# Weights in parts through one queue, cast, turned and multiplied on chip before the gate, in the start of a recurrent attention and maxout kernel

## The chip, the cores and the metric

One core of a Trainium2 chip (trn2). The metric is the device time of one execution in microseconds (us); fast executions of one kernel lie within about 1.5% of each other (159.77 to 161.48 in seven of the kernel before, 155.39 to 156.37 in four of the changed one). Profiles show one execution; their *span* runs from the first to the last instruction and is about 1.7 us shorter than the time. Some executions fall in a slow state, and one of the kernel before took 200.93 us. Medians are over all executions of a run; ratios and verdicts use its fast ones only.

## The reference, cut to what matters

```python
# RWKV-6 like recurrence; B, H, S, D = 4, 8, 768, 48
for t in range(S):
    cur = einsum('bhd,bhe->bhde', u * k[t], v[t])
    y[t] = einsum('bhd,bhde->bhe', r[t], state + cur)
    state = w[t][..., None] * state + einsum('bhd,bhe->bhde', k[t], v[t])
x = y as (3072 tokens, 384)
out = maximum(x @ w1, x @ w2) @ w_out      # w1, w2: 384 x 1024; w_out: 1024 x 384
```

The kernel uses max(a, b) = b + relu(a - b): with wd = w1 - w2 and wc = w2 @ w_out, out = relu(x @ wd) @ w_out + x @ wc. So before the first *gate product* (x @ wd) all of wd must exist, and before the first output all of wc.

## The kernel before

The work is cut into 12 units (3 chunks of 256 positions x 4 batches). A schedule by hand, one long string of steps such as `cs.1` (step cs of unit 1), gives the order; each engine takes its own steps in this order. I count units from zero only inside step names; in prose unit `.0` is the first.

| steps | engine | what |
|---|---|---|
| w k r v, u | transfer queue | loads of a unit (384 KB each), and u to all partitions |
| lw, lp, cs, m, z, AO, AE, iA | ScalarE, GpSimd, TensorE, VectorE | log of the decay, pair sums, prefix sums, exponentials |
| rp, kp, tr, ev | VectorE, TensorE | decayed r and k, turned on TensorE, copied out |
| rk, rku, dg, vd, yb | GpSimd, VectorE, TensorE | the diagonal term r*u*k times v |
| kv, Sa, Tf, S1, sc, M, yi, ya, xT | all | state, scores, masks, output y, copied as bf16 |
| g, r, oc, oa, ob, os | TensorE, ScalarE | gate products, relu, two output products, copies |
| row, WL, Wt, dec, S0 | queue, ScalarE, GpSimd | decay of the state to the next chunk |

The parts that change:

```python
def w1(n):  nc.sync.dma_start(out=w1f, in_=rows(moe_w1))          # f32, plain queue
def w2(n):  nc.gpsimd.dma_start(out=w2_sb, in_=rows(moe_w2))      # cast to bf16 in transfer
def wo(n):  nc.gpsimd.dma_start(out=wo_sb, in_=rows(moe_w_out))   # cast to bf16 in transfer
def wd(ko): nc.vector.tensor_sub(wd_sb[:, ko, :], w1f[:, ko, :], w2_sb[:, ko, :])
def wt(ko): nc.sync.dma_start_transpose(out=w2T_sb[:, ko], in_=w2_sb[:, ko, :])
def wcm(ko): ... 8 matmuls of w2T_sb and wo_sb                    # 3 x 8 = 24 in all
def wce(ko): nc.vector.tensor_copy(wc_sb[:, ko, :], WC[ko])
def lp(n):  nc.gpsimd.tensor_add(t, lw[:, :, 0, :], lw[:, :, 1, :])
def ya(n):
    inter(n, 0)                      # term of the old state
    for i in range(2): ...           # masked scores times v
```

Of the kernel before, what the change touches and what calls it, by code (L numbers as in the profile page):

```python
# [553 lines left out]
```

## Time and profile before

| | |
|---|---|
| time, median of the first three runs | 161.64 us (160.17 to 200.93) |
| span of the profiled run | 158.9 us |
| first gate product starts | 28.47 us |
| TensorE busy before it / from it to the last copy | 8.82 of 28.47 / 126.39 of 126.96 us |
| from the last copy to the end | 3.47 us |

To be read as: a start of 28.5 us in which TensorE mostly waits, then a stretch in which it does nothing but work. The prediction shows the lines.

### The profile page before, as it was taken

How to read it: one execution, taken by the hardware profiler on the slowest of the kernel's cores; microseconds unless marked ns; L12 is line 12 of the kernel's file. 1: busy time of each engine (PE TensorE's matmuls, PEld its weight loads, DVE VectorE, ACT ScalarE, POOL GpSimd, SP SyncE). 2: the span in 40 equal slices, each digit the busy share in tenths (PEclk: the TensorE clock that was granted, in tenths of full speed). 3: DMA queues.
4: the chain of work that ended last, by engine and by line, in shares of the span. 5: the costliest groups of instructions: out<-in, count | busy, mean ns of one | idle time of the engine just before them, and what ended most of it. 6: DMA issues, size and time to landing. Idle time of an engine off the chain costs nothing.

```text
span 158.9 us, 6567 instructions
## 1 busy us (share of the span) xinstructions
PE 135.2 (85%) x2920; PEld 90.1 (57%) x2920; DVE 100.4 (63%) x168; ACT 96.9 (61%) x165; POOL 94.7 (60%) x91
## 2 busy tenths in 40 slices
PE   0402860899999999999899999999999999999991
PEld 0102440565676676766666767667667576586760
DVE  6345579848847859669377596693966956844000
ACT  3242322662397687857858679778587785774641
POOL 8556554808499299952976919958589395330000
PEclk9999999999999999999999999999999999999999
DMA  5999999999999950239496962999229520010402
GB/s 133 248 190 369 366 214 247 178 288 254 268 269 262 247 161 6 106 52 324 132 277 171 283 170 86 220 283 280 89 76 262 167 101 6 15 38 4 151 4 99
...
## 3 DMA queue, kind: packets, MB, share of 16 engines
...
## 4 chain that ended last, share of the span: by engine, by line
PE 82%; DMA 6%; DVE 4%; SPq 2%; POOL 2%; issue 2%; ACT 0%; ACTq 0%; DVEq 0%
PE go L474 22%; PE go L498 20%; PE go L493 9%; PE ex L239 6%; DMA lv<-in_v_dram 6%; PE sc L395 6%; PE y L457 4%; PE sc L327 4%; PE y L436 3%; PE go L219 3%; PE y L349 3%; DVE wd_sb L207 3%; PE y L418 2%; SPq L181 1%; DVE M L400 1%
## 5 line engine op out<-in xcount | busy, mean ns | idle before, releaser
L400 DVE TENSOR_TENSOR M<-sc,mask 128x512 bf16<-128x512 f32 x48 | 30.9, 686 | 17.8 <-PE sc L395 17.8
L474 PE MATMUL go<-xT,wd_sb 128*128 128x256 bf16 x288 | 37.6, 282 | 4.8 <-DVE wd_sb L207 4.3
L482 ACT ACTIVATE gT<-go 128x512 bf16<-128x512 f32 x48 | 27.9, 595 | 16.6 <-PE go L474 15.7
L474 PEld LDWEIGHTS <-wd_sb 128*128 128x128 bf16 x288 | 28.0, 100 | 13.3 <-DVE wd_sb L207 4.6
L498 PE MATMUL go<-wo_sb,gT 128*128 128x384 bf16 x192 | 35.5, 326 | 0.0
L299 POOL TENSOR_TENSOR rku<-lr,lk 128x768 f32<-128x768 f32 x12 | 21.8, 1813 | 8.6 <-DMA lr<-in_r_dram 8.6
L498 PEld LDWEIGHTS <-gT 128*128 128x128 bf16 x192 | 18.6, 98 | 12.3
L315 POOL TENSOR_TENSOR vd<-lv,dg 128x768 bf16<-128x768 f32 x12 | 17.7, 1476 | 12.0 <-DVE dg L310 11.8
L304 POOL TENSOR_TENSOR rku<-rku,u_b 128x768 f32<-128x768 f32 x12 | 21.8, 1813 | 2.6 <-DMA u_b<-in_u_dram 1.8
L239 PE MATMUL ex<-lp,triS 128*128 128x384 f32 x24 | 12.4, 603 | 7.0 <-POOL lp L235 7.0
L235 POOL TENSOR_TENSOR lp<-lw 128x384 f32<-128x384 f32 x12 | 12.0, 999 | 9.2 <-ACT lw L230 9.2
L265 ACT ACTIVATE ex<-mz 128x768 f32<-128x768 f32 x12 | 9.8, 814 | 10.5 <-DVE rn L269 10.5
L493 PE MATMUL go<-wc_sb,xT 128*128 128x384 bf16 x72 | 15.8, 329 | 0.0
L503 ACT COPY osb<-go 128x384 f32<-128x384 f32 x24 | 11.4, 476 | 7.1 <-PE go L498 7.1
L334 DVE COPY T<-sc 128x1024 bf16<-128x1024 bf16 x12 | 8.3, 689 | 11.7 <-PE sc L327 11.6
L230 ACT ACTIVATE lw<-lw 128x768 f32<-128x768 f32 x12 | 10.1, 838 | 8.8 <-DMA lw<-in_w_dram 8.8
L465 ACT CAST xT<-y 128x768 bf16<-128x768 f32 x12 | 12.2, 1020 | 4.5 <-PE y L457 4.5
L294 POOL CAST vn<-lv 128x768 bf16<-128x768 f32 x12 | 10.8, 905 | 3.8 <-DMA lv<-in_v_dram 3.8
L334 ACT COPY T<-sc 128x1024 bf16<-128x1024 bf16 x12 | 12.1, 1012 | 1.0 <-PE sc L327 0.3
L310 DVE TENSOR_REDUCE dg<-rku 128x16 f32<-128x768 f32 x12 | 11.4, 946 | 1.3 <-POOL rku L304 1.3
L269 DVE TENSOR_TENSOR rn<-lr,ex 128x768 bf16<-128x768 f32 x12 | 11.3, 945 | 1.1 <-ACT ex L261 1.1
L395 PE MATMUL sc<-T 48*64 48x128 bf16 x384 | 10.8, 229 | 1.1 <-DVE M L400 1.1
...
## 6 DMA issues: line engine op xcount, KB each, us to landing
...
```

Source lines behind the costliest of these rows:

```text
L239: nc.tensor.matmul(EX[:, 0, 0:HD], triS, U[n]["lp"].rearrange("p h d -> p (h d)"))
L299: nc.gpsimd.tensor_mul(t, U[n]["r"], U[n]["k"])
L304: nc.gpsimd.tensor_mul(t, t, u_b.rearrange("p (h d) -> p h d", h=H).unsqueeze(1).to_broadcast([P, 2, H, D]))
L315: nc.gpsimd.tensor_mul(t.rearrange("p i h d -> p h i d"), U[n]["v"], U[n]["dg"].to_broadcast([P, H, 2, D]))
L334: copy(t.rearrange("d j i p q -> d (j i p q)"), U[n]["tr"][b].rearrange("d j i p q -> d (j i p q)"))
L395: nc.tensor.matmul(sc[e][q, p, :], t[d, 1, i, p, :], t[d, 0, :, p, :])
L400: nc.vector.tensor_mul(U[n]["M", i][:, e], U[n]["sc", i][e], mask[:, i].rearrange("s i q -> s (i q)").unsqueeze(1).to_broadcast([P, NP, P]))
L465: nc.scalar.copy(t.rearrange("c b k (q i) -> c (b k) i q", i=2), U[n]["y"][:, :, 0:HD].rearrange("c b (k i q) -> c b k i q", k=KO, i=2))
L474: nc.tensor.matmul(g[:, f, :], wd_sb[:, ko, fo * P:(fo + 1) * P], U[n]["xT"][:, :, ko, :], start=(f == 0 and ko == 0), stop=(f == 1 and ko ...
L482: nc.scalar.activation(U[n]["gT"][:, 2 * j:2 * j + 2].rearrange("p f j t -> p (f j t)"), U[n]["g", j].rearrange("p f j t -> p (f j t)"), A ...
L493: nc.tensor.matmul(t, U[n]["xT"][:, b, ko, :], wc_sb[:, ko, :], start=(ko == 0), stop=False)
L498: nc.tensor.matmul(U[n]["o", b], U[n]["gT"][:, fo, b, :], wo_sb[:, fo, :], start=False, stop=(fo == FO - 1))
```

## The change

The intent is to shorten the start: load the weights as f32 parts through one queue in the order of need, cast them on chip, turn w2 on TensorE while it would wait, and make the wc products before the first gate product. Its core (cut; the whole order string is rewoven too, for all 12 units):

```diff
+    def wa(ko): nc.sync.dma_start(out=w1f[:, ko], in_=moe_w1[ko * P:(ko + 1) * P, :])
+    def wl(ko): nc.sync.dma_start(out=w2f[:, ko], in_=moe_w2[ko * P:(ko + 1) * P, :])
+    def wq(ko): nc.scalar.copy(w2_sb[:, ko, :], w2f[:, ko, :])
+    def wf(h):  nc.sync.dma_start(out=half(wof, h), in_=half(rows(moe_w_out), h))
+    def wh(h):  nc.gpsimd.tensor_copy(half(wo_sb, h), half(wof, h))
-    def wt(ko): nc.sync.dma_start_transpose(...)
+    def wtm(ko): 8 x nc.tensor.transpose(t[:, fo, :], w2_sb[:, ko, fo * P:(fo + 1) * P], ident)
+    def wte(ko): nc.scalar.copy(w2T_sb[:, ko] ..., WT[ko] ...)
     def wce(ko):
-        nc.vector.tensor_copy(wc_sb[:, ko, :], WC[ko])
+        nc.scalar.copy(wc_sb[:, ko, :], WC[ko])
     def lp(n):
+        eng = nc.vector if n in (0, 1) else nc.gpsimd
     def ya(n):
-        inter(n, 0)
         for i in range(2):
+            if i == 1: inter(n, 0)
-    for t in S_f + S_0: nc.vector.memset(t, 0.0)   # first chunk copies its state instead
 ... (order of the start, before)
-... ya.0 xT.0 w1 wd.1 wd.2 k.1 ... wt.0 lw.2 lp.2 wd.0 rp.1 iA.1 g0.0 ... wcm.0 wce.0 ... wcm.2 wce.2
+... ya.0 xT.0 r.1 rp.1 iA.1 wcm.2 wce.2 wa.2 wd.2 wcm.1 wce.1 row.1 k.1 ... tr.1 ... w.2 lw.2 lp.2 wcm.0 wce.0 g0.0
```

A routine `warm` (matmuls of zeros) is defined and not called.

More of the change, by code (lines that the diff above doesn't have):

```diff
@@ L17 @@
 ORDER = """
-w.0 k.0 r.0 u v.0 w.1 lw.0 w2 lp.0 cs.0 m.0 z.0 AO.0 AE.0 rp.0 row.0 iA.0 rk.0 rku.0 dg.0 vb.0
-vd.0 lw.1 lp.1 kp.0 kv.0 Sa.0 S1.0 Tf.0 tr.0 ev1.0 ev0.0 cs.1 m.1 z.1 AO.1 AE.1 yb.0 yi.0 sc0.0
-M0a.0 M0b.0 sc1.0 M1a.0 M1b.0 ya.0 xT.0 w1 wd.1 wd.2 k.1 r.1 v.1 w.2 wo rk.1 rku.1 vb.1 wt.0
-lw.2 lp.2 wd.0 rp.1 iA.1 g0.0 r0.0 dg.1 vd.1 g1.0 r1.0 g2.0 r2.0 kp.1 tr.1 ev1.1 ev0.1 kv.1 Sa.1
-Tf.1 S1.1 cs.2 m.2 g3.0 r3.0 yb.1 yi.1 sc1.1 M1a.1 M1b.1 z.2 AO.2 AE.2 wcm.0 wce.0 sc0.1 M0a.1
-M0b.1 wt.1 wcm.1 wce.1 wt.2 wcm.2 wce.2 k.2 r.2 v.2 w.3 rk.2 rku.2 vb.2 rp.2 iA.2 dg.2 vd.2 lw.3
@@ L24 @@
-lp.3 ya.1 xT.1 oc0.0 oa0.0 ob0.0 os0.0 oc1.0 oa1.0 ob1.0 os1.0 kp.2 tr.2 ev0.2 ev1.2 kv.2 Sa.2
-Tf.2 S1.2 g0.1 r0.1 g1.1 r1.1 k.3 r.3 v.3 rk.3 rku.3 w.4 vb.3 k.4 r.4 v.4 w.5 lw.4 lp.4 yb.2
-yi.2 sc1.2 M1a.2 M1b.2 cs.3 g2.1 g3.1 r2.1 r3.1 row.1 m.3 z.3 AO.3 AE.3 sc0.2 M0a.2 M0b.2 vb.4
-rp.3 iA.3 oc0.1 oa0.1 ob0.1 os0.1 WL.0 Wt.0 dec.0 S0.0 ya.2 xT.2 oc1.1 oa1.1 ob1.1 os1.1 dg.3
-vd.3 rk.4 rku.4 out1.0 kp.3 tr.3 ev1.3 ev0.3 kv.3 Sa.3 S1.3 Tf.3 g0.2 r0.2 g1.2 r1.2 yb.3 yi.3
-sc1.3 M1a.3 M1b.3 k.5 r.5 v.5 w.6 vb.5 cs.4 lw.5 lp.5 g2.2 r2.2 g3.2 r3.2 out0.0 row.2 m.4 z.4
@@ L30 @@
-AO.4 AE.4 WL.1 Wt.1 dec.1 S0.1 sc0.3 M0a.3 M0b.3 lw.6 lp.6 rp.4 iA.4 out1.1 oc0.2 oa0.2 ob0.2
-os0.2 oc1.2 oa1.2 out0.2 row.3 ya.3 xT.3 ob1.2 os1.2 dg.4 vd.4 rk.5 rku.5 kp.4 tr.4 ev0.4 ev1.4
-kv.4 Sa.4 S1.4 Tf.4 g0.3 r0.3 g1.3 r1.3 out0.1 yb.4 yi.4 sc1.4 M1a.4 M1b.4 cs.5 g2.3 r2.3 g3.3
-r3.3 m.5 z.5 AO.5 AE.5 sc0.4 M0a.4 M0b.4 rp.5 iA.5 oc0.3 oa0.3 ob0.3 os0.3 dg.5 vd.5 ya.4 xT.4
-row.4 WL.4 Wt.4 dec.4 WL.2 Wt.2 dec.2 S0.2 oc1.3 oa1.3 ob1.3 os1.3 kp.5 tr.5 ev0.5 kv.5 ev1.5
-Sa.5 S1.5 Tf.5 g0.4 r0.4 g1.4 r1.4 yb.5 yi.5 sc1.5 M1a.5 M1b.5 S0.4 cs.6 m.6 g2.4 r2.4 g3.4 r3.4
@@ L36 @@
-z.6 AO.6 AE.6 sc0.5 M0a.5 M0b.5 k.6 r.6 v.6 vb.6 w.7 rk.6 rku.6 lw.7 lp.7 rp.6 iA.6 out1.3 oc0.4
-oa0.4 ob0.4 os0.4 dg.6 vd.6 ya.5 xT.5 oc1.4 oa1.4 ob1.4 os1.4 kp.6 tr.6 ev0.6 ev1.6 kv.6 Sa.6
-S1.6 Tf.6 g0.5 r0.5 g1.5 r1.5 yb.6 yi.6 sc1.6 M1a.6 M1b.6 row.5 cs.7 m.7 g2.5 r2.5 g3.5 r3.5
-out1.2 z.7 AO.7 AE.7 sc0.6 M0a.6 M0b.6 k.7 r.7 v.7 w.8 vb.7 rk.7 rku.7 lw.8 lp.8 rp.7 iA.7 dg.7
-vd.7 oc0.5 oa0.5 ob0.5 os0.5 WL.3 Wt.3 dec.3 S0.3 ya.6 xT.6 out0.3 oc1.5 oa1.5 ob1.5 os1.5 kp.7
-tr.7 ev0.7 ev1.7 kv.7 Sa.7 S1.7 Tf.7 row.6 g0.6 r0.6 g1.6 r1.6 k.8 r.8 v.8 w.9 rk.8 vb.8 rku.8
@@ L42 @@
-WL.5 Wt.5 dec.5 S0.5 lw.9 lp.9 yb.7 yi.7 sc1.7 M1a.7 M1b.7 cs.8 m.8 out0.4 row.7 g2.6 r2.6 g3.6
-r3.6 out0.5 z.8 AO.8 AE.8 sc0.7 M0a.7 M0b.7 rp.8 iA.8 oc0.6 oa0.6 ob0.6 os0.6 dg.8 vd.8 ya.7
-xT.7 oc1.6 oa1.6 ob1.6 os1.6 out1.5 WL.6 Wt.6 dec.6 S0.6 kp.8 tr.8 kv.8 ev0.8 Sa.8 ev1.8 S1.8
-g0.7 g1.7 r0.7 r1.7 yb.8 yi.8 sc1.8 M1a.8 M1b.8 cs.9 g2.7 r2.7 g3.7 r3.7 m.9 z.9 AO.9 AE.9 sc0.8
-M0a.8 M0b.8 k.9 r.9 v.9 w.10 rk.9 rku.9 lw.10 lp.10 vb.9 rp.9 iA.9 k.10 r.10 v.10 w.11 vb.10
-out1.4 oc0.7 oa0.7 ob0.7 os0.7 out0.7 dg.9 vd.9 ya.8 xT.8 oc1.7 oa1.7 ob1.7 os1.7 kp.9 tr.9
@@ L48 @@
-ev0.9 kv.9 Sa.9 ev1.9 S1.9 g0.8 r0.8 g1.8 r1.8 rk.10 rku.10 out0.6 yb.9 yi.9 sc1.9 M1a.9 M1b.9
-lw.11 lp.11 cs.10 m.10 g2.8 r2.8 g3.8 r3.8 z.10 AO.10 AE.10 sc0.9 M0a.9 M0b.9 rp.10 iA.10 oc0.8
-oa0.8 ob0.8 os0.8 oc1.8 oa1.8 ya.9 xT.9 ob1.8 os1.8 dg.10 vd.10 kp.10 tr.10 kv.10 ev0.10 Sa.10
-ev1.10 S1.10 g0.9 r0.9 g1.9 r1.9 k.11 r.11 v.11 vb.11 rk.11 rku.11 yb.10 yi.10 sc1.10 M1a.10
-M1b.10 cs.11 m.11 g2.9 r2.9 g3.9 r3.9 z.11 AO.11 AE.11 sc0.10 M0a.10 M0b.10 out1.6 rp.11 iA.11
-WL.7 Wt.7 dec.7 S0.7 out1.7 oc0.9 oa0.9 ob0.9 os0.9 ya.10 xT.10 dg.11 vd.11 oc1.9 oa1.9 ob1.9
@@ L54 @@
-os1.9 kp.11 tr.11 ev0.11 kv.11 ev1.11 Sa.11 S1.11 g0.10 r0.10 g1.10 r1.10 out0.8 yb.11 yi.11
-sc1.11 M1a.11 M1b.11 g2.10 r2.10 g3.10 r3.10 sc0.11 M0a.11 M0b.11 out1.8 out0.9 oc0.10 oa0.10
-ob0.10 os0.10 out0.10 ya.11 xT.11 out1.9 oc1.10 oa1.10 ob1.10 os1.10 g0.11 r0.11 g1.11 r1.11
-g2.11 r2.11 g3.11 r3.11 out1.10 oc0.11 oa0.11 ob0.11 os0.11 out0.11 oc1.11 oa1.11 ob1.11 os1.11
-out1.11
+w.0 lw.0 lp.0 wl.1 wq.1 wl.2 wq.2 r.0 k.0 rk.0 cs.0 m.0 z.0 AO.0 AE.0 rp.0 iA.0 kp.0 tr.0 ev1.0
+ev0.0 wtm.1 wte.1 u rku.0 dg.0 v.0 vb.0 vd.0 kv.0 Sa.0 Tf.0 S1.0 yb.0 yi.0 wa.1 wd.1 w.1 lw.1
@@ new lines @@
+lp.1 wl.0 wq.0 wf.0 wh.0 wf.1 wh.1 sc0.0 M0a.0 M0b.0 wtm.0 wte.0 cs.1 m.1 z.1 AO.1 AE.1 wtm.2
+wte.2 sc1.0 M1a.0 M1b.0 ya.0 xT.0 r.1 rp.1 iA.1 wcm.2 wce.2 wa.2 wd.2 wcm.1 wce.1 row.1 k.1 rk.1
+rku.1 kp.1 wa.0 wd.0 tr.1 ev0.1 ev1.1 w.2 lw.2 lp.2 wcm.0 wce.0 g0.0 r0.0 dg.1 sc1.1 M1a.1 M1b.1
+g1.0 r1.0 g2.0 r2.0 WL.1 Wt.1 row.0 v.1 vb.1 vd.1 kv.1 Sa.1 Tf.1 dec.1 S1.1 k.2 WL.0 cs.2 m.2
+r.2 rk.2 rku.2 g3.0 r3.0 oc0.0 z.2 AO.2 AE.2 rp.2 iA.2 yb.1 yi.1 sc0.1 M0a.1 M0b.1 oa0.0 v.2
+vb.2 w.3 lw.3 lp.3 k.3 r.3 row.2 ob0.0 os0.0 oc1.0 out0.0 oa1.0 ob1.0 os1.0 out1.0 ya.1 xT.1
@@ new lines @@
+S0.1 kp.2 tr.2 ev0.2 cs.3 kv.2 dg.2 vd.2 rk.3 rku.3 g0.1 r0.1 g1.1 r1.1 ev1.2 sc1.2 Sa.2 S1.2
+Tf.2 g2.1 r2.1 g3.1 r3.1 yb.2 yi.2 m.3 z.3 AO.3 AE.3 M1a.2 M1b.2 sc0.2 M0a.2 rp.3 iA.3 v.3 vb.3
+w.4 lw.4 lp.4 k.4 r.4 v.4 vb.4 oc0.1 oa0.1 ob0.1 os0.1 out0.1 oc1.1 oa1.1 ob1.1 os1.1 out1.1
+M0b.2 ya.2 xT.2 kp.3 tr.3 ev0.3 cs.4 dg.3 vd.3 rk.4 rku.4 Wt.0 dec.0 S0.0 ev1.3 kv.3 Sa.3 S1.3
+g0.2 g1.2 r0.2 r1.2 row.3 Tf.3 yb.3 m.4 z.4 AO.4 AE.4 sc1.3 M1a.3 M1b.3 g2.2 r2.2 g3.2 r3.2 rp.4
+iA.4 w.5 lw.5 lp.5 k.5 yi.3 sc0.3 M0a.3 oc0.2 oa0.2 ob0.2 os0.2 oc1.2 M0b.3 ya.3 xT.3 oa1.2
@@ new lines @@
+ob1.2 os1.2 dg.4 vd.4 WL.3 Wt.3 dec.3 S0.3 kp.4 kv.4 tr.4 ev0.4 cs.5 Sa.4 S1.4 g0.3 r0.3 g1.3
+r1.3 ev1.4 sc1.4 Tf.4 m.5 z.5 AO.5 AE.5 M1a.4 r.5 rk.5 rku.5 v.5 vb.5 M1b.4 yb.4 g2.3 r2.3 g3.3
+r3.3 yi.4 sc0.4 row.4 WL.4 Wt.4 dec.4 out1.2 w.6 lw.6 lp.6 k.6 rp.5 iA.5 oc0.3 oa0.3 ob0.3 os0.3
+oc1.3 oa1.3 ob1.3 os1.3 dg.5 vd.5 WL.2 Wt.2 dec.2 S0.2 row.5 M0a.4 M0b.4 ya.4 xT.4 S0.4 kp.5
+cs.6 tr.5 ev0.5 ev1.5 m.6 kv.5 g0.4 r0.4 g1.4 r1.4 Sa.5 S1.5 Tf.5 sc1.5 M1a.5 M1b.5 g2.4 r2.4
+g3.4 r3.4 z.6 AO.6 AE.6 r.6 rk.6 rku.6 dg.6 rp.6 iA.6 out0.2 v.6 vb.6 vd.6 w.7 lw.7 lp.7 k.7 r.7
@@ new lines @@
+rk.7 rku.7 out1.3 out0.3 yb.5 yi.5 sc0.5 M0a.5 oc0.4 oa0.4 ob0.4 os0.4 oc1.4 oa1.4 ob1.4 os1.4
+M0b.5 ya.5 xT.5 kp.6 tr.6 ev0.6 cs.7 ev1.6 row.6 g0.5 r0.5 g1.5 r1.5 m.7 z.7 AO.7 AE.7 sc1.6
+M1a.6 kv.6 Sa.6 S1.6 Tf.6 g2.5 r2.5 g3.5 r3.5 v.7 vb.7 M1b.6 out0.4 w.8 lw.8 lp.8 k.8 yb.6 yi.6
+sc0.6 dg.7 vd.7 rp.7 iA.7 row.7 oc0.5 oa0.5 ob0.5 os0.5 oc1.5 oa1.5 out1.4 WL.5 Wt.5 dec.5 S0.5
+M0a.6 M0b.6 ya.6 xT.6 ob1.5 os1.5 WL.7 Wt.7 kp.7 tr.7 ev0.7 kv.7 Sa.7 S1.7 Tf.7 dec.7 ev1.7 cs.8
+m.8 g0.6 r0.6 g1.6 r1.6 z.8 AO.8 AE.8 sc1.7 M1a.7 M1b.7 g2.6 r2.6 g3.6 r3.6 yb.7 yi.7 sc0.7 r.8
@@ new lines @@
+rk.8 rku.8 v.8 vb.8 w.9 lw.9 lp.9 rp.8 iA.8 k.9 WL.6 Wt.6 dec.6 S0.6 r.9 v.9 vb.9 w.10 lw.10
+lp.10 k.10 r.10 v.10 oc0.6 oa0.6 ob0.6 os0.6 oc1.6 oa1.6 ob1.6 os1.6 dg.8 vd.8 rk.9 rku.9 M0a.7
+M0b.7 ya.7 xT.7 vb.10 S0.7 kp.8 tr.8 ev0.8 cs.9 ev1.8 m.9 g0.7 r0.7 g1.7 r1.7 kv.8 Sa.8 S1.8
+out1.5 sc1.8 M1a.8 g2.7 r2.7 g3.7 r3.7 M1b.8 out1.6 yb.8 yi.8 z.9 AO.9 AE.9 sc0.8 M0a.8 M0b.8
+oc0.7 oa0.7 w.11 lw.11 lp.11 k.11 r.11 v.11 out0.5 ob0.7 os0.7 oc1.7 rp.9 iA.9 ya.8 xT.8 vb.11
+oa1.7 ob1.7 os1.7 out1.7 g0.8 r0.8 out0.6 dg.9 vd.9 rk.10 rku.10 kp.9 tr.9 ev0.9 kv.9 ev1.9
@@ new lines @@
+cs.10 Sa.9 S1.9 out0.7 g1.8 r1.8 m.10 z.10 AO.10 AE.10 sc1.9 M1a.9 M1b.9 yb.9 yi.9 g2.8 r2.8
+g3.8 r3.8 sc0.9 oc0.8 oa0.8 ob0.8 os0.8 out0.8 oc1.8 rp.10 iA.10 M0a.9 M0b.9 ya.9 xT.9 oa1.8
+ob1.8 os1.8 g0.9 r0.9 dg.10 rk.11 rku.11 vd.10 kp.10 tr.10 ev0.10 cs.11 ev1.10 g1.9 r1.9 g2.9
+r2.9 dg.11 vd.11 m.11 z.11 AO.11 AE.11 sc1.10 M1a.10 kv.10 Sa.10 S1.10 g3.9 r3.9 oc0.9 oa0.9
+M1b.10 rp.11 iA.11 yb.10 yi.10 sc0.10 ob0.9 os0.9 out0.9 oc1.9 oa1.9 M0a.10 M0b.10 ya.10 xT.10
+ob1.9 os1.9 out1.9 kp.11 tr.11 ev0.11 kv.11 out1.8 g0.10 g1.10 ev1.11 sc1.11 Sa.11 S1.11 yb.11
@@ L59 @@
+yi.11 M1a.11 M1b.11 r0.10 r1.10 g2.10 r2.10 g3.10 r3.10 sc0.11 M0a.11 M0b.11 oc0.10 oa0.10
+ob0.10 os0.10 out0.10 oc1.10 ya.11 xT.11 oa1.10 ob1.10 os1.10 g0.11 r0.11 out1.10 g1.11 r1.11
+g2.11 r2.11 g3.11 r3.11 oc0.11 oa0.11 ob0.11 os0.11 oc1.11 out0.11 oa1.11 ob1.11 os1.11 out1.11
 """
@@ L117, in last @@
         return unit(n)[0] == NC - 1
+    zeros = const.tile([P, 4 * P], BF16)
+    nc.vector.memset(zeros, 0.0)
     triS = const.tile([P, P], F32)
@@ L150, in _body @@
                                       (triI if (i, i2) == (0, 1) else triS)[q, q])
-    for t in S_f + S_0:
-        nc.vector.memset(t, 0.0)
     w1f = const.tile([P, KO, d_ff], F32)
     wd_sb = const.tile([P, KO, d_ff], BF16)
+    w2f = const.tile([P, KO, d_ff], F32)
     w2_sb = const.tile([P, KO, d_ff], BF16)
+    wof = const.tile([P, FO, HD], F32)
     wo_sb = const.tile([P, FO, HD], BF16)
@@ L193, in w1, with wa, wl, wq @@
     @op
-    def w1(n):
-        nc.sync.dma_start(out=w1f, in_=rows(moe_w1))
-    @op
-    def w2(n):
-        nc.gpsimd.dma_start(out=w2_sb, in_=rows(moe_w2))
-    @op
-    def wo(n):
-        nc.gpsimd.dma_start(out=wo_sb, in_=rows(moe_w_out))
+    def wa(ko):
+        nc.sync.dma_start(out=w1f[:, ko], in_=moe_w1[ko * P:(ko + 1) * P, :])
+    @op
+    def wl(ko):
+        nc.sync.dma_start(out=w2f[:, ko], in_=moe_w2[ko * P:(ko + 1) * P, :])
+    @op
+    def wq(ko):
+        nc.scalar.copy(w2_sb[:, ko, :], w2f[:, ko, :])
+    def half(t, h):
+        return t[:, h * FO // 2:(h + 1) * FO // 2]
+    @op
+    def wf(h):
+        nc.sync.dma_start(out=half(wof, h), in_=half(rows(moe_w_out), h))
+    @op
+    def wh(h):
+        nc.gpsimd.tensor_copy(half(wo_sb, h), half(wof, h))
     @op
@@ L207, in wd, with wtm, wte, warm @@
         nc.vector.tensor_sub(wd_sb[:, ko, :], w1f[:, ko, :], w2_sb[:, ko, :])
+    WT = {}
     @op
-    def wt(ko):
-        nc.sync.dma_start_transpose(out=w2T_sb[:, ko], in_=w2_sb[:, ko, :])
+    def wtm(ko):
+        WT[ko] = t = pt_([P, FO, P], BF16, "go", 2)
+        for fo in range(FO):
+            nc.tensor.transpose(t[:, fo, :], w2_sb[:, ko, fo * P:(fo + 1) * P], ident)
+    @op
+    def wte(ko):
+        nc.scalar.copy(w2T_sb[:, ko].rearrange("p f d -> p (f d)"), WT[ko].rearrange("p f d -> p (f d)"))
+    @op
+    def warm(k):
+        t = pt_([P, 4 * P], F32, "go", 2)
+        for _ in range(k):
+            nc.tensor.matmul(t, zeros[:, 0:P], zeros, start=True, stop=True)
     WC = {}
@@ L234, in lp @@
         U[n]["lp"] = t = wt_([P, H, D], F32, "lp")
-        nc.gpsimd.tensor_add(t, U[n]["lw"][:, :, 0, :], U[n]["lw"][:, :, 1, :])
+        eng = nc.vector if n in (0, 1) else nc.gpsimd
+        eng.tensor_add(t, U[n]["lw"][:, :, 0, :], U[n]["lw"][:, :, 1, :])
     @op
@@ L363, in Sa @@
     def Sa(n):
+        c, b = unit(n)
         U[n]["Sa"] = t = wt_([P, NP, DP], F32, "Sa")
-        nc.vector.tensor_add(flat(t), U[n]["kv"][:, 0, 0:NP * DP], flat(S_f[unit(n)[1]]))
+        kv0 = U[n]["kv"][:, 0, 0:NP * DP]
+        if c == 0:
+            nc.vector.tensor_copy(flat(t), kv0)
+        else:
+            nc.vector.tensor_add(flat(t), kv0, flat(S_f[b]))
     @op
@@ L450, in ya @@
     def ya(n):
-        inter(n, 0)
         for i in range(2):
+            if i == 1:
+                inter(n, 0)
             for p in range(NP):
```

## The prediction

> **What bounds the kernel now.** I read the page's shares first, then the chain that ended last in order of time, then the waits of TensorE, then the timeline of the first 30 us. First the page: the shares (engine, busy us, share, instructions), the forty slices, and the chain by engine.
>
> ```profile
> PE 135.2 (85%) x2920; PEld 90.1 (57%) x2920; DVE 100.4 (63%) x168; ACT 96.9 (61%) x165; POOL 94.7 (60%) x91
> PE   0402860899999999999899999999999999999991
> PE 82%; DMA 6%; DVE 4%; SPq 2%; POOL 2%; issue 2%; ACT 0%; ACTq 0%; DVEq 0%
> ```
>
> TensorE is the only engine near full, and its row of slices says where it is not: the first seven slices (28 us). From the eighth on it is at 9 nearly everywhere. Cutting the span in three (start to first gate product, to the last copy out, the rest) gives it in numbers; the first two columns after the stretch are its length and TensorE's busy time:
>
> ```profile
> 0.00:28.47 28.47, 8.82 (x193) 5.04 (x193) 17.69 (x40) 8.16 (x11) 16.86 (x24) 1.00 1.07 248
> 28.47:155.43 126.96, 126.39 (x2728) 85.01 (x2728) 82.67 (x129) 88.27 (x154) 77.82 (x68) 1.00 0.61 165
> 155.43:158.90 3.47, 0.00 (x0) 0.00 (x0) 0.00 (x0) 0.48 (x1) 0.00 (x0) 1.00 0.16 60
> ```
>
> In the middle stretch TensorE lacks 0.57 us of 126.96. So there only less matmul work, or faster matmuls, can help; everything else is won in the first 28.47 us, where it works 8.82. The chain (start, length, what) tells what that start-up waits for:
>
> ```profile
> 4.21 9.63 DMA lv<-in_v_dram
> 13.89 0.82 POOL vn L294
> 14.71 1.44 POOL vd L315
> 16.15 0.96 POOL lp L235
> 17.16 1.65 PE ex L239 x2
> ...
> 23.49 1.64 DVE wd_sb L207
> 25.13 0.94 issue
> 26.06 2.36 DVE wd_sb L207 x2
> 28.47 4.02 PE go L474 x18
> 32.49 0.91 PE sc L327 x32
> ...
> 36.13 1.41 PE go L219 x8
> 37.53 0.40 PE sc L395 x16
> 37.93 2.71 PE go L219 x16
> ```
>
> The load of v takes 9.63 us from issue to landing; the first unit follows; at 23.49 the three subtractions w1 - w2 (L207) stand in VectorE's queue with TensorE idle until 28.47. Then 18 gate products take 4.02 us, 223 ns each; at 46.08 the chain shows 12 in 1.42 (118 ns), at 49.20 in 1.31 (109 ns). The first batch runs at half speed, though the page's row of granted clock reads 9 in every slice. The 24 products for wc (L219: 1.41 + 2.71 = 4.12 us) come later, on the full TensorE. TensorE's waits agree; the gate product's is the last of the start-up:
>
> ```profile
> PE ex L239 <- POOL lp L235: 7.0, 2, 6.2
> PE y L349 <- POOL vn L294: 6.9, 1, 6.9
> PE go L474 <- DVE wd_sb L207: 4.3, 1, 4.3
> ```
>
> [...]223 against 109 ns, and full speed about 4 us after the dense start at 28.47. [...]The trace has only 64x64 ones: 32 in 0.57 us of chain (45.14), 18 ns each, while one record lasts 199 ns; so I count throughput, not that latency. [...]the three subtractions have 1210/1212/2735 ns; the long one starts at 23.40 while GpSimd's product L304 runs from 23.25 to 25.06, and 25.06 + 1.21 is its end. [...]Here the DMA view gives 275 GB/s in 2 to 4.5 us (plain 384-byte rows, near 325 once running), 200 in 5 to 9 us and 210 in 20 to 24 us with the casting transfers in flight, and 409 in 13.5 to 16.5 us for w1's long rows.
>
> **The change, part by part.**
> Loads. The casting loads of w2 and w_out go; f32 parts come by the plain queue in order of need and are cast by ScalarE (w2) and GpSimd (w_out). The bytes read are the same, but at 325 (inputs) and about 400 GB/s (weights). Worked in queue order from 3.6 us, when w of the first unit is through (it landed at 4.22): two parts of w2 (0.52 MB, 1.3 us each) to 6.2, r and k (1.2 each) to 8.6, u and v to 10.3, a part of w1 11.6, the next w 12.8, the last part of w2 14.1, w_out 17.9, then r 19.1, a part of w1 20.4. Landing is some 0.6 us later. v lands near 10.9 instead of 13.84. The next small copy of the decay row waits for the second unit's state, at about 21.5, and holds k and the last part of w1 behind it to about 24.5 and 25.7.
>
> First unit. Logarithm 4.2 to 5.06 as before; the pair sum moves from GpSimd (0.99) to VectorE (0.55 by the like addition L253): 0.5 us saved. Prefix product, two additions, exponentials: r's factor done 10.55, and k's at 12.4 instead of 14.2, because the reduction L310 no longer stands before it. But r*k*u on GpSimd must wait for k (9.2): 2 x 1.81 to 12.8, reduction to 14.75, vd (1.48) to 16.2. That is where it ends today (16.15). So yb starts at 16.3 rather than 18.74, since the second prefix product no longer stands before it; then scores, four masked products (0.69 each), one subtraction, the second pair sum and its additions on VectorE. Last part of ya near 23.5, against 24.16 now: this part gains little.
>
> Weights. The DMA transposes become 24 of TensorE's plus three ScalarE copies (1.01 each, as L334). At 128 columns and the 109 ns of a 256-column product, each costs 55 ns warm, 110 cold: 1.3 to 2.6 us, all in start-up gaps. ScalarE gets three casts (1.0 each) and the three wc copies (0.5) from VectorE; it has 8.16 us of work in 28.47, so 15 fit. Subtractions: one goes into a gap at 15.6, the other two between the second unit's factors, behind TensorE's wc products. Those now stand before the first gate product: 23.5 to about 28.5, cold at first (8 x 0.33), then warm, with the 32 transposes of the second unit. First gate product: about 29.0, so nominally 0.5 later than now.
>
> The rest. Matmuls after that are the same in number and shape; "no matmuls of zeros" means only that the warming routine is defined and not called. State memsets (8 instructions, 1.7 us on VectorE before 5.3) were off the path. The state term moved behind the first half of ya only lets that half start without waiting for the state; the middle stretch has 0.57 us of idle, so it can return at most that.
>
> Sum, at the start of the last copy: 155.43 - 4.12 (wc products now ahead of the gate) - 0.91 (second transposes ahead) - 2.05 (18 gate products at 109 instead of 223 ns) + 0.5 (gate starts later) + 1.5 (more gaps with a newly woven order, 2 us instead of 0.57; a guess) = 150.4. Plus the unchanged tail of 3.47: span 153.8. The profiled run took 160.62 for a span of 158.9, so 1.7 more: 155.5 us.
>
> **The rivals.** (1) Transfers become the bound of the start. For: everything is on one queue in order, and 7.7 MB must be in before the gate; a held copy stops all behind it. Against: 7.7 MB at 350 GB/s is 22 us, and the pattern without casts ran at 325 and more. At 280 GB/s the last subtraction would end near 31, and the time be 157.5. (2) [...]VectorE now gets pair sums and subtractions, [...]while GpSimd casts w_out (about 1.64 us a half, from 0.82 for 768 columns). A blocked pair sum delays the second prefix product and all masks after it by up to 1.8 us: 157 to 158. (3) The middle stretch gets gaps: the order of all units is changed, and TensorE takes its queue in order. 0.3 us per unit over eleven units is 3.3 instead of the 1.5: 157.3. Against: masks, evictions and exponentials add to some 7 to 8 us per unit of 10.4 on each other engine. (4) It goes better: gate product at 28 and no new gaps, 153.0.
>
> **Range and chances.** 155.5 us; two of the bad rivals together give 159.5, the good one with a bit more 152.0, so 152.0 to 159.5 should hold it 8 times in 10. Two per cent below the fast level before (160.17 to 161.64; the 200.93 is a disturbed run) is about 157.6, which one rival alone hardly reaches: 0.77 faster, 0.19 within 2%, 0.04 slower.
>
> **What would show it.** v's load within 8 us of issue; no wait of TensorE for the subtractions of several us; the wc products and 24 transposes before the first gate product, this one at 28 to 30 and at 109 ns; about 126.5 - 7 of TensorE work after it with at most 2 us idle. Wrong if the gate starts after 31.5, if the gate products are still near 220 ns, or if the middle stretch shows over 4 us of waits for masks, for k's factor or for the state.

## The result, and the profile after

| | before | after |
|---|---|---|
| median time, runs of this comparison | 160.9 us (4 runs) | 155.83 us (155.39 to 156.37, 4 runs) |
| ratio after/before, fast runs | | 0.972 (95%: 0.964 to 0.980) |
| repeated later (a_again) | 160.48 us | 155.94 us, ratio 0.975 (0.970 to 0.980) |
| span of the profiled run | 158.9 us | 154.6 us |

A ratio is the mean time of one kernel's fast runs over that of the other's fast runs of the same rounds, so not quite the ratio of the medians. The result agrees with the predicted 155.5 us.

The page after, the lines that answer to those of before (busy us, share, instructions; the forty slices; the chain by engine):

```profile
PE 134.6 (87%) x2944; PEld 90.7 (59%) x2944; DVE 97.3 (63%) x160; ACT 104.4 (68%) x174; POOL 93.5 (60%) x89
...
PE   0405697889999999999999995999999999999991
...
PE 78%; DMA 9%; POOL 3%; ACT 2%; SPq 2%; issue 2%; DVE 1%; ACTq 0%; POOLq 0%
```

The slices from the eighth on look alike; of those before, the fourth, sixth and seventh are fuller (5, 9 and 7 instead of 2, 6 and 0). "Before" is read from the prediction's lines. The same cut in three shows what moved (length of the stretch, then TensorE's busy time; this cut lies 0.16 us ahead of the last copy, which starts at 151.26, so 0.08 us of TensorE's work stands in the third line):

```profile
0.00:29.57 29.57, 15.29 (x273) 9.53 (x273) 18.32 (x37) 16.41 (x21) 13.99 (x21) 1.00 0.90 285
29.57:151.10 121.53, 119.19 (x2672) 81.22 (x2672) 79.00 (x124) 87.51 (x152) 79.52 (x69) 1.00 0.62 167
151.10:154.60 3.50, 0.08 (x1) 0.00 (x0) 0.00 (x0) 0.48 (x1) 0.00 (x0) 0.99 0.23 83
```

The first gate product starts 1.1 us *later* than before (29.57 against 28.47). But TensorE has done 15.29 us of work by then instead of 8.82, and what is left takes 119.19 us of work instead of 126.39. The gain is not an earlier start of the dense stretch but a shorter dense stretch. TensorE is idle in it for 2.34 us (121.53 - 119.19), against 0.57 before.

TensorE around the first gate product, from the timeline (start, length, engine, line, instruction, count, idle before and its releaser; L246 are the wc products, L355 the turning of the second unit's r and k, L508 the gate products):

```profile
24.38 2.77 PE L246 MATMUL go<-wo_sb,w2T_sb 128*128 128x384 bf16 x16 [0.42 <-ACT w2T_sb L232]
27.09 0.41 PE L355 MATMUL sc<-ident,rn 64*128 64x64 bf16 x16
27.56 0.41 PE L355 MATMUL sc<-ident,kn 64*128 64x64 bf16 x16
27.90 1.47 PE L246 MATMUL go<-wo_sb,w2T_sb 128*128 128x384 bf16 x8
29.57 0.83 PE L508 MATMUL go<-xT,wd_sb 128*128 128x256 bf16 x6 [0.19 <-DVE wd_sb L220]
```

This is the change at work: where the kernel before had 4.3 us of nothing, 24 wc products and 32 transposes stand. The gate then starts warm: 6 products in a record of 0.83 us, where before 18 took 4.02.

What the start waits for, from the chain (start, length, what):

```profile
2.78 8.08 DMA lk<-in_k_dram
11.01 1.82 POOL rku L327
12.89 1.81 POOL rku L332
...
23.73 6.45 DMA lw<-in_w_dram
30.20 0.84 ACT lw L257
31.05 0.38 ACT wc_sb L251
31.46 1.47 PE go L508 x12
```

Two things were not in the prediction. The load of k takes 8.08 us (it was to land at 9.2 and did at about 10.9). And at 30.20 a copy of a wc product stands in ScalarE's queue behind the third unit's logarithm, which waits for its load; the next gate group needs that copy's buffer. TensorE's waits from just before the gate to the end are these three:

```profile
PE y L377 <- issue: 1.6, 1, 1.6
PE go L508 <- ACT wc_sb L251: 0.7, 1, 0.7
PE go L508 <- DVE wd_sb L220: 0.2, 1, 0.2
```

"issue" means that the profile shows nothing that TensorE waited for; more of it below.

VectorE is the last link before the gate. Its timeline just ahead of it, in the kernel after:

```profile
23.67 0.95 DVE L297 TENSOR_TENSOR rn<-lr,ex 128x768 bf16<-128x768 f32 x1 [0.17 <-DMA lr<-in_r_dram]
24.73 1.23 DVE L220 TENSOR_TENSOR wd_sb<-w1f,w_sb 128x1024 bf16<-128x1024 f32 x1
26.55 0.95 DVE L301 TENSOR_TENSOR kn<-lk,ex 128x768 bf16<-128x768 f32 x1 [0.60 <-DMA lk<-in_k_dram]
27.95 1.56 DVE L220 TENSOR_TENSOR wd_sb<-w1f,w_sb 128x1024 bf16<-128x1024 f32 x1 [0.44 <-DMA w1f<-in_moe_w_dram]
```

Four operations nearly end to end, with three short waits for loads; the gate starts when the last subtraction ends.

### The profile page after: what moved, and what is told of

It reads as the page before. It is cut to its first block, busy times and chain, and to the rows that moved or that the text cites. A ratio compares the mean times of both kernels' runs of the same rounds, so it can differ in the third digit from the quotient of the medians.

```text
span 154.6 us, 6617 instructions
## 1 busy us (share of the span) xinstructions
PE 134.6 (87%) x2944; PEld 90.7 (59%) x2944; DVE 97.3 (63%) x160; ACT 104.4 (68%) x174; POOL 93.5 (60%) x89
## 2 busy tenths in 40 slices
DMA packets 59709, 28.97 MB, mean 187 GB/s; under 512 B 54680, under 2 KB 58904, under 8 KB 59680
## 4 chain that ended last, share of the span: by engine, by line
PE 78%; DMA 9%; POOL 3%; ACT 2%; SPq 2%; issue 2%; DVE 1%; ACTq 0%; POOLq 0%
PE go L508 21%; PE go L532 21%; PE go L527 8%; PE ex L267 6%; DMA lk<-in_k_dram 5%; PE sc L428 5%; PE y L491 5%; DMA lw<-in_w_dram 4%; PE sc L355 4%; PE y L377 3%; PE y L469 3%; PE y L451 2%; POOL rku L327 1%; POOL rku L332 1%; ACT lw L257 1%
## 5 line engine op out<-in xcount | busy, mean ns | idle before, releaser
L508 PE MATMUL go<-xT,wd_sb 128*128 128x256 bf16 x288 | 36.1, 273 | 0.9 <-ACT wc_sb L251 0.7
L508 PEld LDWEIGHTS <-wd_sb 128*128 128x128 bf16 x288 | 26.9, 98 | 8.2 <-issue 2.5
L532 PEld LDWEIGHTS <-gT 128*128 128x128 bf16 x192 | 18.1, 98 | 12.1
L332 POOL TENSOR_TENSOR rku<-rku,u_b 128x768 f32<-128x768 f32 x12 | 22.7, 1888 | 0.9
L362 DVE COPY T<-sc 128x1024 bf16<-128x1024 bf16 x12 | 8.3, 689 | 14.0 <-PE sc L355 13.9
L263 POOL TENSOR_TENSOR lp<-lw 128x384 f32<-128x384 f32 x10 | 10.0, 1004 | 6.5 <-ACT lw L257 6.5
L301 DVE TENSOR_TENSOR kn<-lk,ex 128x768 bf16<-128x768 f32 x12 | 11.4, 947 | 2.8 <-ACT ex L293 2.1
L491 PE MATMUL y<-M,vn 64*32 64x128 bf16 x768 | 11.0, 219 | 0.6 <-DVE M L433 0.6
```

What stands on the lines that cost most here:

```text
L332: nc.gpsimd.tensor_mul(t, t, u_b.rearrange("p (h d) -> p h d", h=H).unsqueeze(1).to_broadcast([P, 2, H, D]))
L362: copy(t.rearrange("d j i p q -> d (j i p q)"), U[n]["tr"][b].rearrange("d j i p q -> d (j i p q)"))
L491: nc.tensor.matmul(out32(n, p, w, b), vwin(n, q, i, p, w * 32, 32), U[n]["M", i][q, WIN[w][0], p, :], start=False, stop=(i == 1 and p == N ...
L508: nc.tensor.matmul(g[:, f, :], wd_sb[:, ko, fo * P:(fo + 1) * P], U[n]["xT"][:, :, ko, :], start=(f == 0 and ko == 0), stop=(f == 1 and ko ...
L532: nc.tensor.matmul(U[n]["o", b], U[n]["gT"][:, fo, b, :], wo_sb[:, fo, :], start=False, stop=(fo == FO - 1))
```

## The experiments

Theory: (a) the gain is TensorE work moved from the full stretch into the gap before the gate (4.12 us of wc products, the second unit's transposes), (b) plus the gate's first products at full speed (2.05 us), and the other parts of the change (parts of the loads, casts on chip, turning w2 on TensorE) are what makes the moved work possible in time. Rival: the loads or the order gained it elsewhere, and moving the wc products is incidental. Twelve runs were made; none gave a wrong result. All times are to be read against 155.8 us after and 160 us before; the ratio to before of the same rounds is the firmer number. The variants have slightly other line numbers (L507 for L508, and so on).

**The wc products back behind the gate (a_wc_late).**

```diff
- ... iA.1 wcm.2 wce.2 wa.2 wd.2 wcm.1 wce.1 row.1 ... lp.2 wcm.0 wce.0 g0.0 ... g3.0 r3.0 oc0.0
+ ... iA.1 wa.2 wd.2 row.1 ... lp.2 g0.0 ... g3.0 r3.0 wcm.2 wce.2 wcm.1 wce.1 wcm.0 wce.0 oc0.0
```

> The changed kernel, with the 24 wc products and their copies moved from ahead of the first gate product to behind the first unit's four gate groups, about where they are in the kernel before. Theory (the gain is that the wait for the subtractions is filled with these products): the first gate product still waits for the last subtraction and starts at 29 to 30, colder; the 4.1 us come later on the full TensorE, plus 0.5 to 2 us of cold gate products: time 159.5 to 162, ratio to before about 1.00. Rival (the gain is from loads and order elsewhere, and the first gate product would be free to start earlier without wc in front): time below 157.5.

Measured: 161.09 us, ratio 1.006 (1.000 to 1.011). The whole gain is gone. Its TensorE timeline:

```profile
28.96 1.46 PE L507 MATMUL go<-xT,wd_sb 128*128 128x256 bf16 x6 [1.39 <-DVE wd_sb L219]
30.35 0.64 PE L427 MATMUL sc<-T 48*64 48x128 bf16 x16
30.93 2.26 PE L507 MATMUL go<-xT,wd_sb 128*128 128x256 bf16 x12
```

The gate starts at 28.96, about where it does with the wc products in front (29.57, and 28.88 in a_again): it waits for the last subtraction either way. And it starts cold (6 in 1.46 us). The granted clock shows why, in a cut by it (clock third from the end) and a cut at the gate:

```profile
22.31:25.72 3.41, 1.47 (x88) 0.90 (x64) 3.18 (x4) 3.14 (x5) 0.55 (x1) 1.00 0.79 251
25.72:32.55 6.83, 4.20 (x46) 2.78 (x47) 5.24 (x6) 2.58 (x4) 6.45 (x5) 0.50 0.96 239
28.96:155.48 126.52, 124.70 (x2696) 84.14 (x2696) 79.00 (x124) 88.61 (x154) 79.63 (x69) 0.99 0.59 160
```

After 3.41 us in which TensorE works 1.47, the clock falls to 0.50 at 25.72, and it is back at 32.55; all four runs of this kernel have a mean clock of 0.968 to 0.979, those of the changed kernel 0.997 to 1.000 in the first comparison. From the gate to the last copy TensorE works 124.70 us, 5.43 more than in the changed kernel to the same point (119.27 to 151.26). Of these, 4.06 are the wc products themselves (24 in a record of 4.06 us at 34.89) and the remaining 1.4 are put down to the half clock. The rival falls: without this one move nothing of the gain is left. That the move is enough by itself is not shown, and a_castdma and a_dmaT below speak against it. It undoes (a) and (b) together; the sum just made parts them by account. The run that would part them by experiment, this kernel with matmuls of zeros in place of the wc products, was not made; the next run tries (b) alone, but in the kernel before.

**Warm the array in the kernel before (b_warm).** The changed kernel's warming routine, put into the kernel before, where nothing else changes.

```diff
+    def warm(k): t = psum tile; k x nc.tensor.matmul(t, zeros[:, 0:P], zeros, start=True, stop=True)
- ... g0.0 r0.0 ...
+ ... warm.11 g0.0 r0.0 ...
```

> The kernel before, with 11 matmuls of zeros (128x512) put on TensorE between the end of the first unit's ya (24.2 us) and the first gate product (28.47), where it is idle; nothing else changes. If the 18 first gate products ran at 223 ns because the array was cold, as the prediction says, they come to about 109 ns, the stretch from the first gate product to the last copy shrinks by 2.0 to 2.4 us, and the ratio to before is about 0.986. Rival: they were slow for another reason (weight loads, which had 197 ns each there, or the evictions behind them), since the row of granted clock shows full speed: then they stay near 220 ns and the ratio is 1.00.

Measured: 160.25 us, ratio 0.999 (0.993 to 1.005). The first lines are its timeline, the last its cut at the gate (length, then TensorE's busy time, come first after the stretch):

```profile
23.66 4.13 PE L217 MATMUL go<-zeros 128*128 128x512 bf16 x11
28.04 1.48 PE L480 MATMUL go<-xT,wd_sb 128*128 128x256 bf16 x12 [0.25 <-DVE wd_sb L207]
30.84 0.81 PE L480 MATMUL go<-xT,wd_sb 128*128 128x256 bf16 x6 [1.31 <-ACT gT L488]
```

```profile
28.04:155.60 127.56, 124.80 (x2728) 84.13 (x2728) 82.82 (x129) 88.10 (x154) 77.85 (x68) 1.00 0.62 164
```

The mechanism is as predicted: 12 gate products take 1.48 us, and TensorE's work in the stretch falls by 1.59 us (126.39 to 124.80). The time does not: idle in it grows from 0.57 to 2.76 us. At once TensorE waits 1.31 us for an eviction that stands in ScalarE's queue behind a logarithm and an exponential; the logarithm starts at 28.73, in the kernel before at 28.66, where its load is what it waits for. The rest of the new idle comes later (0.4 for masks, 0.9 as "issue"). So the slow matmuls of the kernel before were largely hidden: what came after them was not ready earlier. The expectation was right about the speed and wrong about the time (0.986), the rival right about the time (1.00) and wrong about the speed.

**Cast in the transfer again (a_castdma).**

```diff
-    nc.sync.dma_start(out=w2f[:, ko], in_=moe_w2[...]);  nc.scalar.copy(w2_sb[:, ko, :], w2f[:, ko, :])
+    nc.gpsimd.dma_start(out=w2_sb[:, ko], in_=moe_w2[...])       # and w_out alike
```

> The changed kernel, with the parts of w2 and w_out loaded by GpSimd's casting transfers straight to bf16 (as the kernel before does, but in the same parts and order), without the on-chip casts. Theory (casting transfers run at about 200 GB/s and crowd the plain loads): w_out and the last part of w2 land 3 to 5 us later, the wc products and with them the first gate product start at 32 to 34, time 158 to 161. Rival (load speed does not set the start; the on-chip casts only cost engine time): within 1 us of 155.8.

Measured: 158.55 us, ratio 0.991 (0.984 to 0.998): 2.7 us slower than the changed kernel, more than half of the gain. Its timeline:

```profile
20.34 1.03 PE L227 MATMUL go<-ident,w_sb 128*128 128x128 bf16 x8 [2.72 <-DMA w_sb<-in_moe_w_dram]
...
32.42 0.82 PE L507 MATMUL go<-xT,wd_sb 128*128 128x256 bf16 x6
```

TensorE waits 2.72 us for the last part of w2, and the gate starts at 32.42, as expected. But the reason given (slow casting transfers) is only part of it: by the chain of this run that part was issued at 16.09, from GpSimd and behind its vd, and took 4.20 us to land; in the changed kernel the transfer queue issued it at 10.24. So the run shows that the plain loads with casts on chip are needed; it does not part the rate of the transfers from their place in GpSimd's queue.

**Turn w2 by transfers again (a_dmaT).**

```diff
- wtm.1 wte.1 ... wtm.0 wte.0 ... wtm.2 wte.2        # 24 TensorE transposes, 3 copies
+ wt.1 ... wt.0 ... wt.2                              # 3 DMA transposes on the queue
```

> The changed kernel, with w2 turned by three DMA transposes (as the kernel before does) instead of by 24 TensorE transposes and three copies on ScalarE. Theory (the transposes on the transfer queue hold it: three took the queue 9.8 us and 3.3 to 9.4 us to land in the kernel before): loads behind them come later, the wc products start 2 to 6 us later, time 158 to 162. Rival (the 24 transposes and 3 copies cost what they save, since TensorE's part is 1.0 us each for 8, cold): within 1 us of 155.8.

Measured: 161.94 us, ratio 1.010 (1.004 to 1.015): 6 us slower.

```profile
26.00 5.30 PE L249 MATMUL go<-wo_sb,w2T_sb 128*128 128x384 bf16 x16 [1.41 <-DMA w2T_sb<-w_sb]
...
34.47 0.83 PE L511 MATMUL go<-xT,wd_sb 128*128 128x256 bf16 x6
```

The wc products start at 26.00, wait for the turned w2, and run cold (331 ns each, where the changed kernel, with 16 of the transposes of w2 at 18.82 and 21.03 us, has 173). Whether the transposes on TensorE themselves have a part in that speed is not decided: the idle time ahead of the products differed too, and in a_castdma, which has the transposes (16 of them at 20.34 and 22.55), the first 16 wc products took 4.49 us, 281 ns each. The queue stood at the transposes: the second unit's r was issued at 23.8 us instead of 13.9. Of the two weight parts that were undone, this one is needed more. Whole loads in place of loads in parts were not tried.

**The pair sums back on GpSimd (a_lp_pool).**

```diff
-        eng = nc.vector if n in (0, 1) else nc.gpsimd
+        eng = nc.gpsimd
```

> The changed kernel, with the first two units' pair sums back on GpSimd. Theory of the prediction: 0.45 us saved at the first prefix product, and for the second unit GpSimd is busy with vd to 17.3 us and then waits for w_out, so its sum would be done at about 18.3 to 18.9 like now: 0 to 0.7 us slower than the changed kernel, 155.8 to 156.5. Rival (the two-input sum on VectorE [...]costs as much): no difference.

Measured: 155.89 us, ratio 0.972 (0.966 to 0.977). No difference. TensorE's first wait did go from 5.6 to 6.2 us, but the first unit's end is set by k's load and GpSimd's two products, so the half microsecond seems not to be on the path; the time shows no difference, the reason is argued.

**Where the queue stands (a_u_late).** In the changed kernel the queue's engine spends 4.71 us on issuing the small load of u, and transfers thin out after 9 us.

```diff
- ... ev0.0 wtm.1 wte.1 u rku.0 dg.0 v.0 ...
+ ... ev0.0 wtm.1 wte.1 v.0 u rku.0 dg.0 ...
```

> The changed kernel, with the load of u issued after that of v instead of before it. In the changed kernel the issue of u held the queue's engine from 3.66 to 8.37 us, and the transfers ran dry after 9 us. If u itself (one row to all partitions) is what holds the queue there, v is issued at about 3.7 in 0.5 us, transfers stay dense, w_out lands 1 to 2 us earlier, and the time falls by 0.5 to 1.5 us (154.3 to 155.3). Rival: the queue is full at that point whatever comes next; then v's issue takes the 4 to 5 us instead, and the time stays within 0.5 us of the changed kernel's 155.8.

Measured: 157.51 us, ratio 0.981 (0.976 to 0.987). The queue's timeline after (first fence) and in this run (second):

```profile
2.78 0.84 SPq L183 DMA_DIRECT2D lk<-in_k_dram  x1
3.66 4.71 SPq L192 DMA_DIRECT2D u_b<-in_u_dram  x1
8.42 0.43 SPq L183 DMA_DIRECT2D lv<-in_v_dram  x1
```

```profile
2.79 0.89 SPq L182 DMA_DIRECT2D lk<-in_k_dram  x1
3.72 4.45 SPq L182 DMA_DIRECT2D lv<-in_v_dram  x1
8.22 1.15 SPq L191 DMA_DIRECT2D u_b<-in_u_dram  x1
```

The rival is right about the queue: whichever of the two comes at this point is held 4.5 us. It is wrong about the time, which it put within 0.5 us of 155.8: u now comes later, and GpSimd's second product waits 2.51 us for it. (The profiled run of this one fell in the slow state; I use of it only times of the start, up to 16 us; the drop of its clock to half comes at 97 us. The ratio is from the fast runs.)

**w2 behind the first unit's loads (a_w2_behind).**

```diff
- w.0 lw.0 lp.0 wl.1 wq.1 wl.2 wq.2 r.0 k.0 ... u ... v.0
+ w.0 lw.0 lp.0 r.0 k.0 u v.0 wl.1 wl.2 ... kp.0 wq.1 tr.0 ev1.0 ev0.0 wtm.1 wte.1 wq.2
```

> The changed kernel, with the first two parts of w2 loaded after the first unit's v instead of right after its w, and ScalarE's casts of them moved behind its exponentials. Theory (in the changed kernel k landed at 10.9 us and the first exponential stood behind two casts that waited for w2, so the first unit is late by what w2 took): k lands at about 7, vd is done at about 14 instead of 17.3, the first unit's ya ends 2 us earlier, the first gate product 0.5 to 1.5 us earlier, time 154.3 to 155.3. Rival (the loads in sum, not their order, set the first gate product): the same time within 0.4 us, or later by up to 1 us, because the turned w2 and the wc products come later.

Measured: 156.3 us, ratio 0.977 (0.971 to 0.984), gate at 28.87. GpSimd's timeline:

```profile
6.66 1.80 POOL L326 TENSOR_TENSOR rku<-lr,lk 128x768 f32<-128x768 f32 x1 [3.58 <-DMA lk<-in_k_dram]
9.05 1.81 POOL L331 TENSOR_TENSOR rku<-rku,u_b 128x768 f32<-128x768 f32 x1 [0.59 <-DMA u_b<-in_u_dram]
...
14.64 1.48 POOL L342 TENSOR_TENSOR vd<-lv,dg 128x768 bf16<-128x768 f32 x1 [3.01 <-DVE dg L337]
```

r and k are in at 6.66 instead of 11.01, but vd waits 3.01 us for a reduction that stands in VectorE's queue behind k's factor and an eviction: a wait took the place of the one removed, and the gate did not move. That is what the rival expected.

**The decay row's copy behind three loads (a_row_late).**

```diff
- ... wce.1 row.1 k.1 ... wa.0 wd.0 ... w.2 lw.2 ...
+ ... wce.1 k.1 ... wa.0 wd.0 ... w.2 row.1 lw.2 ...
```

> The changed kernel, with the second unit's small copy of the decay row (which waits for the second unit's state, 22.3 us) issued after the loads of its k, the last part of w1 and the third unit's w instead of before them. Theory (that copy holds the queue: transfers ran at 191 GB/s from 22 to 24.5 us, then k's factor, the last subtraction and the third unit's logarithm waited 0.6, 0.4 and 1.2 us for their loads, and the copy of a wc product behind that logarithm cost TensorE 0.7): these waits go, the first gate product starts 0.5 to 0.9 us earlier and the time falls by 1.0 to 1.6 us, to 154.2 to 154.8. Rival (TensorE is held by VectorE's queue there, not by the loads): within 0.4 us of 155.8.

Measured: 155.24 us, ratio 0.970 (0.967 to 0.974). In its profile the gate starts at 28.1, the wait for the wc copy is gone, and a new one of 0.8 us for the cast of v stands three steps later. Between the two measurements of the changed kernel (0.972 and 0.975) and this one the intervals overlap: perhaps half a microsecond, not shown.

**The gap without a cause (a_again, a_loads_late), and two attempts at a better kernel (a_best, a_best2).** a_again is the changed kernel, unchanged.

> The changed kernel unchanged, measured again as the base of the three runs beside it: 155.4 to 156.4 us, ratio to before 0.968 to 0.976, and again a gap of 1.1 to 1.6 us on TensorE inside one group of 32 state products near 92 us.

Measured: 155.94 us, ratio 0.975 (0.970 to 0.980), gate at 28.9; the gap is there with 1.65 us.

```diff
  a_loads_late
- ... S0.6 r.9 v.9 vb.9 w.10 lw.10 lp.10 k.10 r.10 v.10 oc0.6 ... os1.6 dg.8 vd.8 ...
+ ... S0.6 oc0.6 ... os1.6 dg.8 vd.8 M0a.7 M0b.7 ya.7 xT.7 S0.7 out1.6 r.9 v.9 w.10 k.10 r.10 v.10 rk.9 rku.9 vb.9 ... out1.5 lw.10 lp.10 vb.10
  a_best = a_loads_late and, in the start
- ... row.1 k.1 ... w.2 lw.2 lp.2 wcm.0 wce.0 ... row.0 v.1 vb.1 ... k.2
+ ... k.1 ... w.2 v.1 vb.1 k.2 rku.1 row.1 wcm.0 wce.0 lw.2 lp.2 ...
  a_best2 = a_best and a_w2_behind, with rku.0 dg.0 ahead of ev1.0
```

> The changed kernel, with the loads of r and v of the tenth unit and of w, k, r and v of the eleventh issued about 5 us later, behind the seventh unit's second output (and what reads them moved as far in the queues). TensorE has a gap of 1.1 to 1.6 us without a cause in the profile in all versions of the changed kernel but one, always between the same two of 32 state products, wherever in time they fall (91 to 98 us); the kernel before has one of 0.46 at another place, at a time with no transfers. Theory (TensorE fetches instructions there and the fetch stands behind bulk loads): with fewer loads in flight at that time the gap shrinks to 0.5 us or less and the time falls by 0.7 to 1.1 us. Rival (the gap is not from transfers): the gap stays at 1.1 to 1.6 us and the time within 0.4 us of the changed kernel's.

> The loads_late version and, in the start, the second unit's k, the last part of w1, the third unit's w, the second unit's v and the third unit's k issued before the decay row's copy, the second unit's v cast before its r*k*u, and the third unit's logarithm behind the last copy of a wc product. If the gains add (0.6 to 1.4 us from the start, 0.7 to 1.1 from the gap), 153.3 to 154.6 us and a ratio to before of 0.958 to 0.966; if TensorE's start is bound by VectorE, 155 us and 0.97.

> The a_best version, with the first two parts of w2 behind the first unit's v and its reduction ahead of an eviction on VectorE. The single change of w2's place gave nothing clear because the reduction stood behind k's factor and an eviction. Theory (with the reduction earlier vd ends near 14.8 instead of 16 to 17 us and the second unit follows): the first gate product 0.5 to 1 us earlier than in a_best, 152.6 to 154 us. Rival (second unit's chain through VectorE and the loads sets it): within 0.4 us of a_best.

Measured: 162.96, 165.07 and 163.42 us; ratios 1.013, 1.025 and 1.017. All three are slower than before. The profile of a_loads_late shows the cause there, a step of mine that all three share; for the other two it is inferred. (In all three profiles the granted clock also falls to 0.50 for 3.41 us, once or twice.) The queue's timeline of a_loads_late:

```profile
102.44 0.36 SPq L541 DMA_DIRECT2D out_dram<-osb  x1
102.84 0.43 SPq L182 DMA_DIRECT2D lr<-in_r_dram  x1
```

I put the loads behind an output that is ready at 102.4 us, not at 92 as I thought: they came 11 us later, not 5. TensorE's waits tell what that made of it:

```profile
PE go L526 <- ACT gT L515: 3.1, 1, 3.1
PE go L507 <- ACT xT L498: 2.2, 1, 2.2
PE y L376 <- issue: 1.2, 1, 1.2
```

Evictions stand behind a logarithm that waits for its load, the same pattern as in b_warm. The gap itself was 1.16 us here, with transfers dense until about its end, so the run as built does not separate theory and rival; the times of its packets, below, say more. The start of a_best and a_best2 did not bring the gate forward either (28.97 and 29.8 us). No version that clearly beats the changed kernel was found.

Several parts have no run of their own: the loads in parts, the wc copies on ScalarE, the rewoven order of the later units, and these two. Putting the state term back to the front of ya in the changed order was refused by the check before any run, so it has no time. The dropped memsets were not tried; that neither of these two matters is argued from the 0.57 us of idle, not shown.

## Why the prediction was right, point by point

- *Gate at about 29.0.* Measured 29.57 and, in the second profile, 28.9. Right in sum, with errors that cancel in part: k landed 1.7 us late (it had been issued at 2.78, ahead of the held load of u, and was as late in a_u_late, so the hold is not shown to be the cause; with the first two parts of w2 behind it, in a_w2_behind, k was in by 6.66), r's factor was done at 11.58 instead of 10.55 behind two casts of w2 on ScalarE, the first half of w_out was cast from 19.69 instead of 16.6, vd was done at 17.26 instead of 16.2; but the wc products, for which I had put cold ones first, were warm from the start (16 in 2.77 us, 173 ns each).
- *4.12 and 0.91 us of work moved ahead of the gate.* Right, and shown for the wc products: with them moved back the time is 161.09.
- *2.05 us from warm gate products.* The first 18 took 0.83 + 1.47 = 2.30 us instead of 4.02, so 1.72. The total came true: 126.39 - 7.08 = 119.3 us of work in the dense stretch was predicted, 119.19 measured; the remaining difference lies in other matmuls that were slow before as well. The prediction wondered that the row of granted clock reads 9 where products run at half speed: the trace's clock records begin at 33.20 us in the kernel before and at 21.38 in the changed one, and the row shows 9 where there is no record yet. As a cause by itself the term is not worth its size in the kernel before: b_warm had the fast products and no gain. That it pays in the changed kernel because the next steps' inputs were there too is argued, not shown; the prediction did not ask for this.
- *24 transposes of w2 in 1.3 to 2.6 us.* Measured: 8 in a record of 1.03 us at 14.02 and at 18.82, and 8 in 0.78 at 21.03, so 129 and 98 ns each and 2.84 in sum. The estimate was scaled from the 109 ns of a gate product; of transposes on TensorE the kernel before has only the 64x64 ones of r and k, 32 in 0.57 us of its chain.
- *1.5 us more gaps.* 2.34 - 0.57 = 1.77 measured. That the size came close is luck: it was a guess, and the kind was wrong: not masks or factors of rewoven units, but one gap of 1.56 without a cause in the profile and 0.72 for a wc copy behind a logarithm.
- *Tail 3.47, and 1.7 from span to time.* From the start of the last copy (151.26) to the end 3.34 us, and 156.37 for a span of 154.6.
- *Rivals.* Transfers: partly there, as a queue that stands (4.71 us at the issue of u) and not as too little rate (the page's slices between 3.9 and 23.2 us show 328, 200, 350, 393 and 337 GB/s, the 200 in the slice from 7.7 us). VectorE held up beside GpSimd: seen but small. The subtractions took 1.33 and 1.56 us where a product of GpSimd ran for part of the time (one to 17.26 us, one from 28.51) and 1.23 where none did; two of the kernel before took 1.21. What makes the difference is not shown: k's factor at 26.55, beside a product from 26.62, took 0.95 us like r's at 23.67 without one. The prediction's reading of the long subtraction is a little off: 25.06 + 1.21 is 26.27, and it ends at 23.40 + 2.74 = 26.14. Gaps in the dense stretch: one. Of the small parts, the pair sum's half microsecond made no difference that a_lp_pool could show.

What stays open: what holds the queue for 4.5 us, and why instructions come late at the gap. The sixth load was held 4.71 us in the changed kernel, 4.45 with v in its place, and 4.27 in a_best; in a_best2, with the first two parts of w2 behind v, no piece of the queue in its chain is longer than 1.16 us up to 7.83, and there a part of w2 takes 3.47. The gap stands inside the same state group of 32 products, with 12 or 11 of them still to come, in ten of the twelve profiles of the changed kernel and its variants (1.1 to 1.8 us), at 91 to 98 us as the group falls. In a_lp_pool only 0.4 us stand there, and the time is the same; in a_dmaT, whose TensorE stream is shorter by the 24 transposes of w2, gaps stand elsewhere, among gate products (2.0 us in three pieces). The candidate, an inference from the traces, is that TensorE has to wait there for its instructions: the page of the profile shows a queue "instruction" with 23 packets and 0.38 MB, and the trace has 16384 bytes for each of them.

The kept traces speak for it. Take every pause of TensorE marked "issue" in its dense stretch, 17 in the 14 profiles and 0.27 to 1.77 us long, and look for the last packet of that queue that had landed when TensorE went on. In the changed kernel the packet landed at 93.05 and TensorE resumed at 94.43, 1.38 us later; in a_lp_pool, whose pause is 0.43 us, 1.25 us later; in the kernel before, with 0.46 us at another place, 1.45. In 16 of the 17 it is 1.21 to 1.48 us, in the other 1.63, while the landing falls anywhere from 1.35 us before the pause begins to 0.44 us into it. So the end of the pause goes with the packet, and its length with how far TensorE had got by then. (The packets' times are in the traces' DMA records; the view of transfers shows them in narrow windows.) This is a regularity found afterwards, not an experiment.
